# The first batch of a delta-net kernel: rounds of two and four tiles, state per head half, smaller transfers

## The chip, the cores and the metric

The kernel runs on one core of a Trainium2 chip. A core has five engines that run side by side: TensorE (PE, matrix products), VectorE (DVE), ScalarE (ACT), GpSimd (POOL) and SyncE (SP, which here only issues DMAs). TensorE reads from the on-chip memory SBUF and writes into PSUM, which has eight banks; VectorE and ScalarE copy its results back ("evictions"). DMAs bring data from the main memory. The metric is the time of one execution on the device in microseconds (us); less is better.

## The reference

Two blocks follow one another. The first is a delta-rule attention over 4 batches of 8 heads, 768 positions and a head width of 48; the state of a head is 48 x 48:

```python
k_n = k / (np.linalg.norm(k, axis=-1, keepdims=True) + 1e-06)
for t in range(S):
    kt, vt, bt = (k_n[:, :, t], v[:, :, t], beta[:, :, t, None])
    y[:, :, t] = np.einsum('bhd,bhde->bhe', q[:, :, t], state)
    v_old = np.einsum('bhde,bhd->bhe', state, kt)
    state = state + bt[:, :, :, None] * np.einsum('bhd,bhe->bhde', kt, vt - v_old)
```

The second takes the heads side by side as rows of 384, mixes them, and adds an MLP of width 1536:

```python
X = np.fft.fft(x, axis=1)
X = np.fft.fft(X, axis=2)
u = x + np.real(X).astype(np.float32)
un = (u - mu) / np.sqrt(var + 1e-06)        # mean and variance over the 384
ch = np.maximum(un @ w_ch1, 0.0) @ w_ch2
return (u + ch).astype(np.float32)
```

The weights come as 64-bit floats, and the kernel makes 32-bit ones of them on the chip.

## The kernel before

**Tiles.** A batch has 6 tiles of 128 positions, in all 24 *units*. A unit holds two chunks of 64 positions, one in partitions 0 to 63, the other in 64 to 127. For each unit the keys are transposed (`turn`, L571 in the profile), multiplied with themselves (`keys` for the first batch), and a triangular matrix per head is inverted. The inversion runs on VectorE over a whole *round* of units at once: the 32 x 32 matrices of up to four units lie side by side, and its cost is that of four, however many there are. The first batch has two rounds, units 0 to 3 and 4 and 5; all others have three units. For the first batch `begin16` (L876 to L942) transposes a round's blocks (L902), takes norms on ScalarE (L909, L911), scales (L928), masks (L935), and `invert16` makes 14 steps of a product (L962) and a sum (L968), a scaling (L981) and transpositions back (L986, L990). `join` and `blocks` put the inverse together per unit.

**The chain of the first batch.** `chain0` goes through 12 chunks one after the other. A chunk subtracts the state's product from its values (`f1`), copies the values out (`g1`), adds their products with the keys to the state in its own PSUM bank (`f2`, bank `bS`), and copies the state out (`g2`) for the next chunk. `fq` and `outputs0` make the outputs. State and values are *joined* here: the state of two heads is kept as one 128 x 96 block with zeros off its diagonal (`so_`, in the tile R1), the values of both chunks as one block (`ub_`, in the tiles u and st), so a product covers two heads, or two chunks, at once. The zeros are cleared once on POOL.

**Mixing and MLP.** When the last tile of a batch is done, `mixing` folds the rows, multiplies with tables for the Fourier transform (`tab`, `ft`), normalizes, and the MLP follows in 12 groups of 2.6 us on TensorE for two tiles. `weights` loads the 64-bit weights in 18 pieces of 512 columns, through buffers in ws, x and R, and converts each in six operations on ScalarE (L2017, L2023), VectorE (L2020, L2028, L2036) and POOL (L2033).

**The order of the work.** Nothing runs in the order of the program text. Each operation is recorded (`Plan.op`) with its engines, an estimated duration, a due time and what it reads and writes. `Plan.schedule` then plays the kernel through on the host and fixes one order for each engine; the engines run these orders in sequence and wait for one another by semaphores. Constants at the top of the file (`GAP`, `FORCE`, `LIM`, `START`, `LATER` and others) steer its choices, and `KEYS` gives small shifts to the due times, a number for every 64 operations. Where TensorE has no work ready, `schedule` puts in *fillers*, matmuls with unused results: up to `E2` = 5 us groups of six 64-column ones (L2263), later one of 256 columns or two (L2270). They are placed only up to `D1`, and where fewer columns than `TARGET` a microsecond were streamed over the last `SPANW` us, or nothing is ready within `GAP`; after `D1` only if nothing is ready. `fetch` estimates when the next 256 instructions of TensorE are there; `crowd` gives its delay by transfers. `pace` ties DMAs on SP's queue to an instruction before them.

The lines that all operations share: L568 is every matmul, L571 every transposition, L577, L579 and L581 every plain copy by ScalarE and VectorE, and L615 every load.

## Time and profile before

| | |
|---|---|
| median of 3 runs | 649.18 us (648.48 to 651.63) |
| profiled execution | 648.84 us, its span 647.0 us |
| TensorE busy | 632.9 us (98%) |
| VectorE busy | 507.3 us (78%) |
| ScalarE busy | 271.6 us (42%) |
| moved by DMA | 31.98 MB |

The profile's page gives for one execution the busy time of each engine, the span in 40 slices, the DMA queues, the chain of work that ended last, and the costliest groups of instructions. PE is TensorE's multiplying, PEld its loading of the stationary operand; a matmul of 32-bit floats shows as two records of each kind. A busy PE need not do useful work: fillers count as well. "Granted clock" is the share of TensorE's full clock. A group's row gives line, engine, operation, output and inputs with shapes, count, busy time and the mean of one in ns.

### The profile page before, as it was taken

The page shows a single profiled execution, that of the slowest core. Times are in us where ns is not written, and L with a number is a line of the kernel's source. Part 1 is how long each engine was busy: PE and PEld are TensorE (multiplying, and loading weights), DVE is VectorE, ACT ScalarE, POOL GpSimd, SP SyncE. Part 2 cuts the span into 40 slices and gives each one's busy share as a digit, 9 for nine tenths or more (in the row PEclk, how much of TensorE's full clock was granted, in tenths as well). Part 3 has the DMA queues.
Part 4 walks back from the last instruction along what each step waited for, and adds up shares of the span by engine and source line. Part 5 has one row for each costly group of instructions (what it writes and reads, how often), then busy time and mean ns, then how long its engine had stood idle before and what let it go on. Part 6 is the DMA issues. An engine that isn't in the chain of part 4 may idle for free.

```text
span 647.0 us, 22705 instructions
## 1 busy us (share of the span) xinstructions
PE 632.9 (98%) x9748; PEld 516.6 (80%) x9748; DVE 507.3 (78%) x1529; ACT 271.6 (42%) x804; POOL 39.8 (6%) x44
## 2 busy tenths in 40 slices
PE   9998899999999999999999999999999999999998
PEld 8788788777777877877777777877777699899997
DVE  4998779999997379999863899999828633976573
ACT  3769665543154544421655333345442113321120
POOL 4103313230000000000000000000000000000000
PEclk9999889999999999999999999999999999999999
DMA  6654534550013231000323220000000000000000
GB/s 126 142 161 134 123 100 110 135 152 2 25 28 87 54 64 27 25 1 2 71 46 64 52 51 2 23 5 3 3 27 3 2 24 1 26 2 25 2 25 24
DMA packets 82808, 31.98 MB, mean 49 GB/s; under 512 B 75667, under 2 KB 79732, under 8 KB 82580
## 3 DMA queue, kind: packets, MB, share of 16 engines
q1 hardware_dynamic: 82516, 30.31, 19.3%
q8 instruction: 76, 1.25, 0.8%
q10 hardware_dynamic: 192, 0.23, 0.2%
q14 instruction: 24, 0.20, 0.1%
HBM read 25.81 MB, written 4.72 MB: 47 GB/s over the span
## 4 chain that ended last, share of the span: by engine, by line
PE 77%; DVE 15%; ACT 4%; issue 2%; DMA 1%; DVEq 0%; ACTq 0%
PE pp L568 72%; PE pp L571 3%; DVE rr L1056 2%; DVE tmp L1051 2%; PE pp L2270 1%; PE pp L2263 1%; ACT us L577 1%; DMA ws<-in_moe_w_ch_dram 1%; DVE gd L812 1%; DVE w L968 1%; ACT w L2017 1%; DVE tmp L962 1%; DVE R L1453 1%; DVE rr L902 1%; DVE w L2036 1%
## 5 line engine op out<-in xcount | busy, mean ns | idle before, releaser
L568 PE MATMUL pp<-R,w 128*128 128x256 f32 (+1 forms) x832 | 182.2, 367 | 0.7 <-DVE us L789 0.7
L568 PEld LDWEIGHTS pp<-R,w 128*128 128x128 f32 x832 | 145.6, 190 | 20.2 <-DVE us L789 0.9
L568 PE MATMUL pp<-w,R 128*128 128x384 f32 x384 | 134.6, 495 | 0.0
L577 ACT ACTIVATE us<-pp 32x128 f32<-32x128 f32 (+3 forms) x232 | 73.1, 348 | 87.4 <-PE pp L568 65.2
L568 PEld LDWEIGHTS pp<-w,R 128*128 128x128 f32 x384 | 70.2, 190 | 41.3
L1697 ACT ACTIVATE R<-pp 128x512 f32<-128x512 f32 x47 | 28.1, 597 | 102.3 <-PE pp L568 92.8
L568 PE MATMUL pp<-us 64*64 64x64 f32 (+4 forms) x2784 | 67.1, 231 | 0.0
L568 PEld LDWEIGHTS pp<-us 64*64 64x64 f32 (+2 forms) x2784 | 56.9, 132 | 5.8 <-issue 3.2
L1056 DVE TENSOR_TENSOR rr<-rr,tmp 128x84 f32<-128x84 f32 (+13 forms) x180 | 57.7, 335 | 1.5
L1051 DVE TENSOR_TENSOR tmp<-rr 128x84 f32<-128x84 f32 (+14 forms) x180 | 57.2, 332 | 1.4
L577 ACT ACTIVATE R<-pp 128x192 f32<-128x192 f32 (+8 forms) x103 | 29.7, 332 | 29.5 <-PE pp L568 18.4
L568 PEld LDWEIGHTS pp<-u,us 64*64 64x64 f32 (+2 forms) x1248 | 29.0, 129 | 15.6 <-issue 10.2
L577 ACT ACTIVATE x<-pp 64x192 f32<-64x192 f32 x91 | 28.3, 323 | 27.4 <-PE pp L568 24.0
L1362 DVE TENSOR_TENSOR u<-u,pp 64x192 f32<-64x192 f32 x66 | 22.1, 349 | 18.8 <-PE pp L568 14.5
L1391 DVE TENSOR_TENSOR st<-st,pp 128x192 f32<-128x192 f32 x30 | 10.5, 351 | 33.5 <-PE pp L568 30.4
L1872 DVE TENSOR_TENSOR us<-us,pp 128x256 f32<-128x256 f32 x64 | 26.8, 420 | 12.3 <-ACT us L577 10.8
L2270 PE MATMUL pp<-pack 64*64 64x256 f32 (+1 forms) x198 | 35.0, 396 | 0.1
L568 PE MATMUL pp<-u,us 64*64 64x48 f32 (+3 forms) x1248 | 34.5, 217 | 0.0
L568 PE MATMUL pp<-st,us 48*64 48x48 f32 (+2 forms) x1184 | 29.5, 223 | 2.6 <-issue 1.1
L568 PEld LDWEIGHTS pp<-st,us 48*64 48x64 f32 (+2 forms) x1184 | 25.0, 135 | 8.3 <-issue 4.9
L1828 DVE TENSOR_TENSOR gd<-us 128x128 f32<-128x128 f32 x48 | 11.8, 289 | 21.8 <-ACT us L1904 15.4
L568 PE MATMUL pp<-us,gd 128*128 128x192 f32 x144 | 27.8, 327 | 0.0
(176 smaller groups left out, 999.6 us busy)
## 6 DMA issues: line engine op xcount, KB each, us to landing
out_dram<-x SPq DMA_DIRECT2D x11, 384.0 KB
us<-in_k_dram SPq DMA_DIRECT2D x16, 192.0 KB
us<-in_q_dram SPq DMA_DIRECT2D x16, 192.0 KB
us<-in_v_dram SPq DMA_DIRECT2D x16, 192.0 KB
us<-in_k_dram SPq DMA_DIRECT2D x8, 181.5 KB
us<-in_q_dram SPq DMA_DIRECT2D x8, 181.5 KB
us<-in_v_dram SPq DMA_DIRECT2D x8, 181.5 KB
x<-in_moe_w_ch_dram SPq DMA_DIRECT2D x3, 484.0 KB
```

What stands on the lines that cost most here:

```text
L568: I(nc.tensor.matmul(o, lhsT=lhsT, rhs=rhs, start=start, stop=stop, skip_group_check=True))
L571: I(nc.tensor.matmul(o, lhsT=src, rhs=ident[p0:p0 + n, p0:p0 + n], is_transpose=True, start=start, stop=True, skip_group_check=True))
L577: I(nc.scalar.activation(o, i, ACT.Copy, **({} if scale is None else {"scale": scale})))
L812: I(nc.vector.scalar_tensor_tensor(w[0], w[1], (m1, m0)[s], w[2], op0=ALU.mult, op1=ALU.add))
L1051: I(eng(e).tensor_tensor(T_, R[:, :, j + 1:32, j:j + 1].broadcast_to([128, ns, n, j]), R[:, :, j:j + 1, 0:j].broadcast_to([128, ns, n, j]) ...
L1056: I(eng(e).tensor_tensor(R[:, :, j + 1:32, 0:j], R[:, :, j + 1:32, 0:j], T_, op=ALU.add))
L1362: I(nc.vector.tensor_tensor(U[:, s], U[:, s], psum(b1[s])[a, s0:s1].rearrange("p (j d) -> p j d", d=D), op=ALU.subtract))
L1391: I(nc.vector.tensor_tensor(sn[:, s0:s1], so[:, s0:s1], psum(b2)[:, s0:s1], op=ALU.add))
L1697: I(nc.scalar.activation(o, s, ACT.Relu))
L1828: vec(128, lambda e, j=j, i0=i0, i1=i1, op=op: I(nc.vector.tensor_tensor(s(j), i0, i1, op=op)), [aH] + rd, [aS(j)], pr - P.ev)
L1872: vec(256, lambda e: I(nc.vector.tensor_tensor(o, i0(), i1(), op=ALU.add)), [], [aH] + list(wr), pr - P.ev, use=n)
L2270: I(nc.tensor.matmul(pst[two[0]][x, 0:256], lhsT=w[x, 0:n], rhs=w[x, 0:256], start=True, stop=True, skip_group_check=True))
```

## The change

The first batch's rounds become units 0 and 1, and units 2 to 5. The state and the values are no longer joined: each head has its 48 x 48 state, two heads of a pair lie in the two halves of the partitions, and products are taken head by head; a chunk's state is copied out by one copy of 128 partitions instead of two of 64, the outputs of a tile by two copies instead of four. In `begin16` the mask is applied before the scale. The zeros in w1 and w2 are cleared in three pieces, and the blocks `GF` of units 2 to 5 lie in w2, those of units 0 and 1 in w1. The table is loaded in four transfers of 32 partitions, the weights in pieces of at most 256 columns (`CUT`). In the planner an opening filler is estimated longer and denser, transfers to start earlier (`MOVED`, `SOON`), `crowd` has another form, the operations that the splits add do not shift the numbering of `KEYS` (`extra`), and nearly all constants and all `KEYS` have new values. With them the opening has two groups of fillers.

```diff
-KEYS = [200, 0, 229, 328, 801, 352, 821, 0, 842, 785, 803, 67, 960, 0, 214, 0, 515, 0, 672, 136, 248, 318, 992, 108, 919, 0, 112, 914, 121, 808, 205, 0, 783, 131, 491, 744, 856, 533, 168, 25, 743, 718, 0, 282, 642, 114, 361, 40]
+KEYS = [0, 196, 0, 882, 0, 533, 747, 349, 300, 92, 0, 631, 0, 118, 229, 329, 112, 81, 189, 0, 488, 857, 205, 426, 209, 734, 514, 433, 0, 264, 416, 0, 634, 135, 91, 0, 140, 556, 752, 279, 934, 886, 297, 564, 670, 480, 0, 737]
...
-LOOK, EARLY = 1e9, 19.0271
-FOLD, BY, SEQ, HOT, HOTPE, HOTPK, HOTG, NORM = 1, 1, 1, 1.7459, 0, 0, 0, 1
-HOTC, PORT, E2 = 1, 1, 5.0
-GAP, HALF = 0.3228, 84.0008
+LOOK, EARLY = 1e9, 0.6403
+FOLD, BY, SEQ, HOT, HOTPE, HOTPK, HOTG, NORM = 1, 1, 10, 5.6131, 8, 12, 1, 1
+HOTC, PORT, E2 = 2, 1, 5.0
+GAP, HALF = 0.2477, 85.6671
...
-FORCE = 621.6309
-BLOCK, LEAD, SEEK, LAND, LAND2, HOLDUP = 256, 60, 1.0, 2.3968, 1.964, 1.8
-PACE, PGAP, MOVED = 3.8256, -0.0594, 1.6
-PACED, AHEAD = 6.0, 0.4
-CUT, ROW = 512, 121
+FORCE = -320.3215
+BLOCK, LEAD, SEEK, LAND, LAND2, HOLDUP = 256, 60, 1.0, 2.0432, 1.8604, 1.0
+PACE, PGAP, MOVED = 6.0, -0.4268, -0.7
+PACED, AHEAD, SOON = 6.0, 0.4, 0.8
+CUT, ROW = 256, 121
...
-TARGET, SPANW = 745.8691, 1.1196
-E0, E1, D1 = 1.0, 10.0, 105.9979
+TARGET, SPANW = 768.6683, 4.0822
+E0, E1, D1 = 1.0, 10.0, 266.9663
...
-        return min(1.0, sum(max(0.0, min(z, t + 1.5) - max(a, t - 0.5)) for a, z in self.bursts) / 2.0)
+        return min(2.6, 0.55 * max([0.0] + [z - t for a, z in self.bursts]))
...
-                        best.engs, best.new, best.banks, best.succ = {"PE": 0.432}, [], [], []
+                        best.engs, best.new, best.banks, best.succ = {"PE": 0.65 if now < E2 else 0.432}, [], [], []
...
-            g, go = (w2, 2304 + 512 * u) if u < 4 else (w1, 3584 + 512 * (u - 4))
+            g, go = (w1, 3584 + 512 * u) if u < 2 else (w2, 2304 + 512 * (u - 2))
...
+        def mask(e):
+            I(nc.vector.tensor_tensor(DB, RB, tri[:, None].broadcast_to(sh), op=ALU.mult))
+        vec(512, mask, [aTRI, aR], [aD], pr, port=True)
...
-        def mask(e):
-            I(nc.vector.tensor_tensor(DB, DB, tri[:, None].broadcast_to(sh), op=ALU.mult))
-        vec(512, mask, [aTRI], [aD], pr, port=True)
...
         if n and 0 in part:
             def f1(e):
-                for j in order:
-                    y, k = j // 2, 64 * (2 * j % 4)
-                    mm(psum(z.bU[c])[64 * y:64 * y + 64, k:k + 128].rearrange(
-                        "p (s d) -> p s d", s=2)[:, :, 16 * y:16 * y + D], z.TK[:, c, j, :],
-                       so[:, 96 * j:96 * j + 96].rearrange("p (s d) -> p s d", s=2), False)
+                for j, s, r in jj:
+                    y = 64 * (c ^ s)
+                    mm(psum(z.bU[s])[y:y + 64, 64 * j:64 * j + 64], z.TK[r, c, j, :],
+                       so[r, D * j - wide(j):D * j - wide(j) + 64], False)
...
-        for s in range(2):
-            def g2(e, s=s):
-                w = psum(bS)[64 * s:64 * s + 64, 0:256]
-                copy(e, sn[64 * s:64 * s + 64, :].rearrange(
...
+        P.op(narrow(W), lambda e: copy(
+            e, sn.rearrange("p (i j d) -> p i j d", i=2, d=D), own0(bS)), [], [A(sn, 0, W)],
+             pr - P.ev - 5, use=[bS], lat=LA)
...
-    rounds = [units[0:4], units[4:6]] + [units[6 + sum(SIZES[:i]):6 + sum(SIZES[:i + 1])] for i in range(len(SIZES))]
+    rounds = [units[0:2], units[2:6]] + [units[6 + sum(SIZES[:i]):6 + sum(SIZES[:i + 1])] for i in range(len(SIZES))]
...
-    for i, (w, n) in enumerate(((w2, 4352), (w1, 4608))):
-        c0 = 3584 if i == 1 else 0
+    for i, (w, c0, n) in enumerate(((w2, 0, 2048), (w1, 3584, 4608), (w2, 2304, 4352))):
+        if i == 2:
+            P.extra.append(len(P.ops))
...
-    for t in ub_ + tuple(so_):
-        nk = t.shape[1]
-        P.op({"POOL": 0.1 + 1.0e-3 * nk}, lambda e, t=t: I(eng(e).memset(t, 0.0)), [], [A(t, 0, nk)], -20,
-             lat=LP)
...
-    dma(tab, cn["tab"].ap().rearrange("p t c -> p (t c)"), [A(tab, 0, 1)], 0, kb=1180)
+    for x in range(0, 128, 32):
+        if x:
+            P.extra.append(len(P.ops))
+        dma(tab[x:x + 32], cn["tab"].ap().rearrange("p t c -> p (t c)")[x:x + 32], [A(tab, 0, 1, x, x + 32)], 0,
+            kb=295)
```

More of the change, by code (lines that the diff above doesn't have):

```diff
@@ L511 @@
     ws = sb("ws", 1024)
[L512 to L513 removed]
+    us_ = [sb(f"u{i}", DM) for i in range(3)]
     lo_ = [sb(f"lo{i}", 256) for i in range(2)]
@@ L593, in either, with narrow @@
         return {"ACT": t_act(n) + w, "DVE": t_dve(n) + 0.06}
+    def narrow(n):
+        return {"ACT": t_act(n) + 0.10, "DVE": t_dve(n) + 0.09}
     T_IN, T_EIGHT, T_RATE = 2.0, 8, 170.0
@@ L1263, in chain0 @@
-            P.op({"PE": T_FQ}, fq, [z.aQT(), A(so, 0, DM)] + ([A(sn, 0, DM)] if n > 1 else []),
-                 [], pr - 4, "64", new=z.bO, lat=LE, col=1536, ni=32)
-            P.op({"ACT": 0.08, "DVE": 0.1}, lambda e: copy(
-                e, mv_[0][:, 14:15], psum(z.bO)[:, 0:1]), [], [A(mv_[0], 14, 15)], pr - P.ev,
-                 use=[z.bO], lat=LA)
+                for j, s, r in jj:
+                    for y, t in ((1, so), (0, sp)):
+                        if 2 * z.T + y:
+                            mm(psum(z.bO[s])[64 * y:64 * y + 64, 64 * j:64 * j + 64],
+                               z.QK[r, 0, y, j, :], t[r, D * j - wide(j):D * j - wide(j) + 64],
+                               j == 0)
@@ L1268, in chain0 @@
+            P.op({"PE": 0.55}, fq, [z.aQT(), A(so, 0, W)] + ([A(sp, 0, W)] if n > 1 else []),
+                 [], pr - 4, "64", new=z.bO, lat=LE, col=1024, ni=64)
+            for s in range(2):
+                P.op({"ACT": 0.08, "DVE": 0.1}, lambda e, s=s: copy(
+                    e, mv_[s][:, 14:15], psum(z.bO[s])[:, 0:1]), [], [A(mv_[s], 14, 15)], pr - P.ev,
+                     use=[z.bO[s]], lat=LA)
         if n and 0 in part:
             def f1(e):
-                for j in order:
-                    y, k = j // 2, 64 * (2 * j % 4)
-                    mm(psum(z.bU[c])[64 * y:64 * y + 64, k:k + 128].rearrange(
-                        "p (s d) -> p s d", s=2)[:, :, 16 * y:16 * y + D], z.TK[:, c, j, :],
-                       so[:, 96 * j:96 * j + 96].rearrange("p (s d) -> p s d", s=2), False)
```

161 lines of the change are left out of this document (73 added, 88 removed).

## The prediction

> **What bounds the kernel now.** I read the page first, then the busy time by stage, the chain of work that ended last, and single groups.
>
> ```profile
> span 647.0 us, 22705 instructions
> PE 632.9 (98%) x9748; PEld 516.6 (80%) x9748; DVE 507.3 (78%) x1529; ACT 271.6 (42%) x804; POOL 39.8 (6%) x44
> ```
> ```profile
> 24.60:37.00 12.40, 12.20 (x280) 8.60 (x279) 12.40 (x67) 5.75 (x20) 1.87 (x6) 1.00 0.68 154
> ...
> 75.00:90.00 15.00, 13.28 (x276) 11.03 (x273) 8.91 (x22) 10.07 (x27) 5.65 (x3) 0.77 0.43 104
> ...
> 102.00:121.00 19.00, 17.70 (x165) 15.86 (x164) 18.81 (x53) 10.01 (x30) 4.17 (x2) 1.00 0.53 126
> ```
> ```profile
> 121.00:267.00 146.00, 144.49 (x2330) 109.68 (x2323) 125.64 (x354) 62.89 (x186) 9.87 (x8) 1.00 0.25 58
> 121.00:647.00 526.00, 520.04 (x7312) 420.69 (x7304) 406.14 (x1208) 191.31 (x569) 10.49 (x10) 1.00 0.13 31
> ```
>
> Columns of the stages: from and to; then length, and busy time (and instructions) of PE, its weight loads, VectorE, ScalarE and POOL; granted clock, DMA share, GB/s. After 121 us TensorE is busy for 520.0 of 526 us: that stage is its own work and moves only if the orders leave more or fewer holes. Before 121 us PE also reads as busy, but much of it is filler that keeps the clock up (below), while VectorE is full at 24.6 to 37 us and again at 102 to 121 us. So the time is the fixed 526 us plus whenever the front lets the first MLP matmul go. The front is where this change works. Its chain:
>
> ```profile
> 1.18 7.20 PE pp L2263 x84
> 8.38 0.39 PE pp L571 x8
> 8.77 0.49 PE pp L2078 x6
> ...
> 10.32 0.39 PE pp L571 x8
> 10.71 0.62 PE pp L568 x32
> ...
> 14.83 0.45 ACT gd L577
> ...
> 16.11 0.49 DVE gd L748
> 16.62 1.96 DVE rr L902
> ...
> 21.91 0.68 DVE w L928 x2
> ...
> 22.93 0.55 DVE w L935
> ...
> 35.10 0.67 DVE w L981 x2
> 35.90 0.98 DVE gd L986
> ```
>
> Columns: start, duration, what. The chain starts with 84 filler matmuls (line 2263) that last 7.20 us; the first real work, the transposition of tile 0's keys (L571), starts when they are through. Nothing was waited for there but the filler in front of it in TensorE's queue.
>
> **The change, part by part.** *Two opening filler groups.* A group is 6 matmuls, 12 records, so 84 records are 7 groups. Is tile 0's key block there earlier? Bytes by microsecond:
>
> ```profile
> 2.00:3.00 1.00, 1.00 (x12) 1.00 (x12) 0.82 (x6) 0.99 (x2) 1.00 (x3) 1.00 0.87 206
> 3.00:4.00 1.00, 1.00 (x12) 1.00 (x11) 0.00 (x0) 0.17 (x1) 1.00 (x1) 1.00 1.22 296
> ```
> ```profile
> 1.00:6.00 5.00, 4.82 (x47) 4.82 (x47) 1.00 0.91 187
> 6.00:8.00 2.00, 2.00 (x38) 2.00 (x37) 1.00 1.07 214
> ```
> ```profile
> us<-in_k_dram SPq DMA_DIRECT2D x16, 192.0 KB
> pack<-k_pack ACTq DMA_DIRECT2D x1, 130.0 KB
> x<-in_beta_dram ACTq DMA_DIRECT2D x1, 96.0 KB
> ```
>
> Identity table, beta and tile 0's keys are 418 KB; 26 KB (of the microsecond before these rows) plus 206 plus 63% of 296 make that at about 3.6 us. From the last byte to the release I allow 1 us (no row shows it; 0 to 3 are the bounds): 4.6 us. The second fence is the fillers alone (line 2263): 47 in 4.82 us, 103 ns each, until 6 us, then 38 in 2.00, 53 ns. The clock was at half until about 6 us although the granted clock reads 1.00. Two groups, 24 at 103 ns, end at 1.18 + 2.5 = 3.7 us, so the keys now set the start: 4.6 instead of 8.38. But TensorE is then cold, and the real work doubles: two turns 0.78 each, beta 0.98, two key products 1.24 each, 5.0 in all, to 9.6 us. The same products of tiles 0 and 1 end in the chain above at 10.71 + 0.62 + 0.39 + 0.62 = 12.3 (tile 2's turn stands between them). Gain 2.7. The other four tiles at 1.01 each end at 13.6 where they ended at 16.5 (row below, 15.34 + 1.16): 2.9. If the cold state lasted through all six, they would cost 4 us more and this gain would turn into a loss of 1; if it were warm, 5.
>
> ```profile
> 15.34 1.16 PE L568 MATMUL pp<-us 48*64 48x64 f32 x64
> ```
>
> The rule that speaks against fewer fillers is the Trainium skill's, TensorE: Matmul & The Clock Gate, What's actually happening: half rate by default, full rate after a busy window of some 3.4 us, and half rate again after an idle one. The trace agrees in size: a mean clock of 0.77 over 15 us is 6.9 us at half rate, two such windows. By that rule the opening could stay cold for one window more, 3.4 us longer than the 4.6 us start suggests; the estimate by it would be about 1.7 us less gain.
>
> *Rounds of two and four; mask first.* A round's inversion on VectorE costs the same for any number of tiles up to four:
>
> ```profile
> L968 DVE TENSOR_TENSOR w<-w,tmp 128x28 f32<-128x28 f32 (+6 forms) x28 | 5.8, 243 | 0.0
> L962 DVE TENSOR_TENSOR tmp<-w 128x28 f32<-128x28 f32 (+6 forms) x28 | 5.8, 242 | 0.0
> ```
>
> 11.6 us for both rounds, 5.8 for one. Now they run interleaved and the first block to be joined is there at 36.9 us. The first round needs four tiles' keys before its transposition at 16.62; a round of two needs two: 9.6 plus two evictions on ScalarE (L577, 0.45 each) and, beginning behind the first, two on VectorE (L748, 0.49 each), 11.4 if they follow one another with nothing between. From there 1.96 for the transposition; an allowance of 1.2 for the root and reciprocal, whose tiny instructions lie hidden in the chain (from its end at 18.58 to the scale at 21.91 at most, 3.3, most of which VectorE spent on the other round); 0.68 for the scale; the mask, 0.55, has moved ahead of it and now runs during the root; 5.8; 0.67; 0.98: the first joinable block at 22.7 alone, at 29 if the second round's own evictions (4 x 0.49), transposition, scale, mask and a turn's copies or two, about 6, go between, against 36.9. The second round's end depends on VectorE's total, which is the same; it moves by the 2.8 that the opening gives. The path into the MLP lies between 2.8 (VectorE full to the end) and 8 (the chain of tiles alone). I take 4, near the lower bound, since VectorE is full in the row 24.6 to 37.
>
> *Unjoined state.* Per tile, 4 value copies, 4 state copies (two per step), 4 output copies and a probe become 4, 2, 2 and two probes. PE's passes are twice as many and half as wide; I cost them at 0 (bounds -2 and +2): 8 records of 128x96 take 0.55 us, 16 of 64x64 about as long (0.68).
>
> ```profile
> 67.50 0.55 PE L568 MATMUL pp<-R 128*64 128x96 f32 x8
> 68.22 0.68 PE L568 MATMUL pp<-t,us 64*64 64x64 f32 x16 [0.17 <-ACT R L577]
> ```
> ```profile
> L577 ACT ACTIVATE R<-pp 64x192 f32<-64x192 f32 x20 | 6.5, 324 | 2.1 <-PE pp L568 1.7
> ```
> ```profile
> L579 DVE COPY st<-pp 64x192 f32<-64x192 f32 x6 | 2.1, 355 | 2.1 <-PE pp L568 2.0
> ```
>
> A copy costs 0.324 on ScalarE and 0.355 on VectorE, and I take the same for 128 partitions of 192 (bounds one and two of them). Over six tiles 70 copies become 47, and 6 more probes of one column are left out as small: 23 x 0.33 = 7.6 us of both engines. Of the copies in these two rows VectorE has 6 of 26: its share is 1.8. On the chain of steps the state's two copies, mostly on one engine one behind the other, become one: 11 x 0.33 = 3.6. Between 1.8 and 3.6 I take 2.7.
>
> *Smaller transfers.* Weight pieces of 256 columns instead of 512 make 24 more issues on SP's queue, the table in four 3 more. 27 at 0.29 are 7.9 us, spread over 110 us in which the queue mostly waits for its pacing.
>
> ```profile
> L615 SPq DMA_DIRECT2D x<-in_moe_w_ch_dram x24: 268/291/328, 38.5 to 133.7; - x24
> L615 SPq DMA_DIRECT2D tab<-k_tab x2: 421/539/657, 52.2 to 139.8; - x2
> ...
> L568 PEld LDWEIGHTS pp<-tab,R x48: 160/163/164, 94.5 to 109.2; 128*96 128x96 f32 x24, 128*97 128x97 f32 x12, 128*95 128x95 f32 x12
> ```
>
> The table is issued at 52.2 and first read at 94.5: hidden. I cost this part at 0; without its cover, 7.9. One case of a late transfer is in the trace, and shows the price of a stall:
>
> ```profile
> 76.03 0.66 ACT L2017 ACTIVATE w<-ws 128x512 f32<-128x512 f32 x1 [2.45 <-DMA ws<-in_moe_w_ch_dram]
> ```
>
> ScalarE waited 2.45 us for weights with the next state copy queued behind it, TensorE for that copy, and the clock fell: 13.28 us busy at 0.77 is 3.1 lost. Together some 5 us. A new order may miss it or meet another; 0, bounds -5 and +5.
>
> The Trainium skill, DMA: Bandwidth & Descriptors, Bandwidth, asks for transfers of 1 MiB and more and gives each a fixed 2 us; paid one after the other, 27 of them would be an estimated 54 us. The trace does not bear out that they add: the opening's key blocks, 192 KB each, came at 187 GB/s over 1 to 6 us, first latency included, and at 214 over 6 to 8, queued one behind the other.
>
> *The rest.* Four clears on POOL go, the clear of w2 is cut in two, the filler slots move between w1 and w2: POOL is 6% busy, 0. *Orders anew* for the long stage: its holes are 6.0 us of idle and 8.8 us of fillers (line 2270 below), so -7 at best; I take 0.
>
> Sum: 4.0 + 2.7 = 6.7, from the profiled run's 648.84 (span 647.0 and 1.84 around it; 0.34 under the median): 642.1, so 642.
>
> **The rivals.** *The front is given back.* The MLP starts when the last work of a full VectorE and the paced weights are through; both are placed by the order, not by the chain. For it: 18.81 of 19 us at 102 to 121. Against: VectorE is idle for over 6 of the 15 us at 75 to 90. Then only the copies' 1.8 come, and less: 647 to 649.
>
> *Fillers in the long stage (slower).* The filler window now reaches to 267 us instead of 106, and its measure is 4.1 us long. Rows of line 2270:
>
> ```profile
> 110.00:121.00 11.00, 2.65 (x8) 1.20 (x8) 1.00 0.53 136
> 121.00:647.00 526.00, 8.80 (x32) 5.42 (x32) 1.00 0.13 31
> ```
>
> Fillers in front of ready work cost what they last. At the rate of 110 to 121 us, 146 us would hold 35 us of them; against this, PE has only 1.5 us of holes there, so the measure should seldom ask. Half of it, 17.5, gives 660; it decides from a fifth on, 6.7 us, where the gain is used up. With a third, 11.7, the time is 654.
>
> *Weights late (slower).* The 7.9 us of added issues come in front of the last pieces, and the gain is lost with them: 657. Against: the queue's pacing leaves room.
>
> **How the numbers follow.** Forecast 0.58; given back 0.18; fillers or a worse order of the long stage 0.16; weights late 0.08. About 0.5% (3.2 us) is what a measurement can tell from no change: below 645.9 is faster, above 652.4 slower. Some of the forecast's mass lies in that band and a little of the given-back case beyond it: faster 0.58, same 0.2, slower 0.22. The forecast's own range is 634 (chain in full, 8 + 3.6, and no stall) to 646 (opening cold, copies 1.8); with the slower cases up to 655.
>
> **What would show it.** 24 opening fillers; first L571 before 5.5 us; first L902 near 11; the first L986 before 30; copies of 128x192 for the state; first MLP matmul (128x256, of the weights) near 114 instead of 121; the same 526 us behind it. Wrong if the turns start late in spite of fewer fillers (landing, not queue), if the clock stays low past 12 us, or if fillers of line 2270 show behind 121 us.

## The result, and the profile after

The changed kernel took 645.01 us (median of 13 runs, 640.33 to 648.18), the kernel before 648.96 (13 runs, 646.76 to 651.63). The ratio is 0.9933, 95% interval 0.9905 to 0.9961: some 4 us faster, where 6.7 were forecast. The ratios leave out executions more than 1.5% above the fastest of their kernel (three in all, in the experiment with fewer fillers). The profiled execution took 647.48 us with a span of 645.6, so it is one of the slower ones: its span is only 1.4 us shorter than the 647.0 before. On two other chips, in the experiments below, the same kernel had 0.9894 (0.9858 to 0.9929) and 0.9857 (0.9817 to 0.9898). The first and the last of these intervals do not overlap, and single executions lie 10 us apart (637.7 to 648.2): that spread has to be explained along with the gain.

Line numbers have moved a little: L568 is now L561 (matmuls), L571 is L564 (transpositions), L577 and L579 are L570 and L572 (copies), L2263 and L2270 are L2260 and L2267 (fillers), L902 and L986 are L895 and L979, L2017 is L2013 (weights).

The opening on TensorE, from the timeline of the changed kernel (start, duration, engine, line, operation, tiles, shapes, count, and in brackets the wait):

```profile
1.18 2.82 PE L2260 MATMUL pp<-pb 128*64 128x64 f32 x24 [1.18 <-DVE pb L686]
4.51 0.69 PE L564 MATMUL pp<-pack,us 64*128 64x64 f32 x8 [0.50 <-DMA us<-in_k_dram]
...
5.90 1.54 PE L2260 MATMUL pp<-pb 128*64 128x64 f32 x12
...
7.99 1.13 PE L561 MATMUL pp<-us 48*64 48x64 f32 x32
...
16.70 1.13 PE L561 MATMUL pp<-us 48*64 48x64 f32 x32
...
18.46 1.06 PE L561 MATMUL pp<-us 48*64 48x64 f32 x28
```

The 24 fillers are there, and the first turn starts at 4.51 after a wait for the load, as forecast (4.6). A third opening group, of 12 records, stands behind the first turn and beta (the third row), where the text on the change counts two groups in all. But a key product takes 1.13 us all the way to 19.5, against 0.69 in the same view of the kernel before: the clock, which was to be released near 9.6, stays at half. The last pair's products end at 19.5 instead of 16.5.

To account for the rest I use two marks: the first copy of a chunk's values (u from pp, the entry into the chain of states) and the first MLP matmul. Both, before and then after:

```profile
49.52 0.72 DVE L579 COPY u<-pp 64x192 f32<-64x192 f32 x2
```
```profile
121.22 5.45 PE L568 MATMUL pp<-R,w 128*128 128x256 f32 x24
```
```profile
46.29 0.37 DVE L572 COPY u<-pp 64x192 f32<-64x192 f32 x1
```
```profile
116.53 5.34 PE L561 MATMUL pp<-R,w 128*128 128x256 f32 x24
```

The entry is 3.23 earlier. From there to the MLP it is 70.24 instead of 71.70, 1.46 less. From the MLP's start to the end of the span it is 529.1 instead of 525.8, 3.3 more. Together 1.4, the difference of the spans.

Two places inside show where it went. ScalarE waits for weights with a state copy queued behind it, and TensorE for that copy (first fence: timeline of ScalarE; second: TensorE's waits from 40 to 121 us, as total, times, longest):

```profile
73.31 0.67 ACT L2013 ACTIVATE w<-ws 128x512 f32<-128x512 f32 x1 [3.45 <-DMA ws<-in_moe_w_ch_dram]
```
```profile
PE pp L561 <- ACT st L570: 3.3, 1, 3.3
PE pp L561 <- issue: 3.0, 5, 0.8
```

And in the long stage TensorE stops in the middle of a gram product, with nothing to wait for that the profile shows, and the clock falls behind it (stages: length, busy times, then granted clock, DMA share, GB/s):

```profile
204.07 1.40 PE L561 MATMUL pp<-us 48*64 48x128 f32 x48 [1.65 <-issue]
```
```profile
200.00:205.00 5.00, 3.35 (x194) 3.01 (x191) 3.31 (x10) 2.92 (x10) 0.00 (x0) 0.97 0.67 161
205.00:215.00 10.00, 10.00 (x280) 8.41 (x276) 2.68 (x8) 5.20 (x18) 0.00 (x0) 0.67 0.13 26
```

Ten microseconds at 0.67 are 3.3 lost, and the wait adds 1.65. The whole stage is only 3.3 longer, so a part of it is made good elsewhere. In the same stretch the kernel before had a clock of 1.00 and no hole.

### The profile page after: what moved, and what is told of

Same layout as the page of the kernel before. It is cut to its first block, busy times and chain, and to the rows that moved or that the text cites. A ratio compares the mean times of both kernels' runs of the same rounds, so it can differ in the third digit from the quotient of the medians.

```text
span 645.6 us, 23067 instructions
## 1 busy us (share of the span) xinstructions
PE 625.0 (97%) x9900; PEld 511.9 (79%) x9900; DVE 512.1 (79%) x1524; ACT 269.0 (42%) x791; POOL 35.9 (6%) x42
## 3 DMA queue, kind: packets, MB, share of 16 engines
q1 hardware_dynamic: 84742, 30.31, 19.3%
## 4 chain that ended last, share of the span: by engine, by line
PE 77%; DVE 15%; DMA 3%; ACT 2%; issue 2%; SPq 0%; DVEq 0%; ACTq 0%
PE pp L561 71%; PE pp L564 3%; PE pp L2267 3%; DVE tmp L1044 3%; DVE rr L1049 3%; ACT us L570 1%; DMA us<-in_k_dram 1%; DVE w L2032 1%; DVE us L782 1%; DVE gd L805 1%; DVE rr L851 1%; DVE R L1449 1%; DMA ws<-in_moe_w_ch_dram 1%; DMA x<-in_moe_w_ch_dram 1%; DMA tab<-k_tab 1%
## 5 line engine op out<-in xcount | busy, mean ns | idle before, releaser
L561 PE MATMUL pp<-R,w 128*128 128x256 f32 (+1 forms) x832 | 184.7, 370 | 0.2 <-DVE us L782 0.2
L561 PEld LDWEIGHTS pp<-R,w 128*128 128x128 f32 x832 | 146.9, 192 | 19.6 <-DVE us L782 0.3
L561 PE MATMUL pp<-w,R 128*128 128x384 f32 x384 | 134.8, 494 | 0.0
L570 ACT ACTIVATE us<-pp 32x128 f32<-32x128 f32 (+3 forms) x240 | 75.9, 349 | 81.0 <-PE pp L561 58.0
L561 PEld LDWEIGHTS pp<-w,R 128*128 128x128 f32 x384 | 69.9, 190 | 40.7 <-issue 0.2
L561 PE MATMUL pp<-us 64*64 64x64 f32 (+4 forms) x2784 | 70.4, 236 | 2.2 <-issue 1.6
L561 PEld LDWEIGHTS pp<-us 64*64 64x64 f32 (+2 forms) x2784 | 59.9, 138 | 8.2 <-issue 3.3
L1044 DVE TENSOR_TENSOR tmp<-rr 128x30 f32<-128x30 f32 (+9 forms) x180 | 58.0, 331 | 2.0
L1049 DVE TENSOR_TENSOR rr<-rr,tmp 128x108 f32<-128x108 f32 (+9 forms) x180 | 57.0, 325 | 2.0
L561 PEld LDWEIGHTS pp<-u,us 64*64 64x64 f32 (+1 forms) x1472 | 37.5, 132 | 17.5 <-issue 10.3
L561 PE MATMUL pp<-u,us 64*64 64x48 f32 (+2 forms) x1472 | 43.9, 219 | 2.2 <-issue 1.6
L570 ACT ACTIVATE R<-pp 128x192 f32<-128x192 f32 (+6 forms) x82 | 22.8, 336 | 31.0 <-PE pp L564 19.6
L561 PE MATMUL pp<-st,us 48*64 48x48 f32 (+1 forms) x1232 | 28.7, 224 | 2.3 <-issue 0.8
L561 PEld LDWEIGHTS pp<-st,us 48*64 48x64 f32 x1232 | 24.3, 136 | 8.0 <-issue 4.3
L570 ACT ACTIVATE x<-pp 64x192 f32<-64x192 f32 (+1 forms) x78 | 24.0, 323 | 15.4 <-PE pp L561 13.0
L570 ACT ACTIVATE u<-pp 64x192 f32<-64x192 f32 (+1 forms) x71 | 23.2, 326 | 15.6 <-PE pp L561 11.3
L561 PE MATMUL pp<-us,gd 128*128 128x192 f32 x144 | 27.8, 327 | 0.0
L1424 DVE TENSOR_TENSOR x<-x,pp 64x192 f32<-64x192 f32 x66 | 23.2, 352 | 4.6 <-PE pp L561 2.8
```

The source lines that it names most:

```text
L561: I(nc.tensor.matmul(o, lhsT=lhsT, rhs=rhs, start=start, stop=stop, skip_group_check=True))
L570: I(nc.scalar.activation(o, i, ACT.Copy, **({} if scale is None else {"scale": scale})))
L1044: I(eng(e).tensor_tensor(T_, R[:, :, j + 1:32, j:j + 1].broadcast_to([128, ns, n, j]), R[:, :, j:j + 1, 0:j].broadcast_to([128, ns, n, j]) ...
L1049: I(eng(e).tensor_tensor(R[:, :, j + 1:32, 0:j], R[:, :, j + 1:32, 0:j], T_, op=ALU.add))
L1424: I(nc.vector.tensor_tensor(w, w, v, op=ALU.add))
```

## The experiments

All compare with the kernel before on their own chip. The kernels below that move operations do it in the finished order, so that nothing else is planned anew.

**The changed kernel again, twice.** No edit.

> The changed kernel once more, for a second profile. If the 1.65 us of issue wait in the gram products near 202 and the clock of 0.50 to 0.84 behind it belong to this order of work (three loads of 384, 192 and 192 KB issued within 3.4 us, with the fetch of instructions behind them), a wait of 1 us or more stands again within 201 to 205 and the stretch 205 to 215 has a clock under 0.9. If they are chance of the one execution, they are gone, and the span is some 3 to 5 us shorter with the first MLP matmul unchanged near 116.5. The wait of ScalarE for the weights at 70 (3.45 us) is expected again within 1 us in either case.

> The changed kernel a third time, beside the two kernels below on the same chip. One of two openings is expected: clock released near 4.6, key products of the last pair ended at 13.7, first state copy at 43.7; or not released before 17, 19.3 and 49.1. The times of its executions spread over 5 us or more, between 638 and 648.

Measured: 641.16 us (637.86 to 644.69), and 639.94 (637.73 to 641.94); the spread of the latter is 4.2 us, not 5 or more. The opening of the first repetition:

```profile
4.26 0.53 PE L564 MATMUL pp<-pack,us 64*128 64x64 f32 x8 [0.25 <-DMA us<-in_k_dram]
...
6.44 0.69 PE L561 MATMUL pp<-us 48*64 48x64 f32 x32
...
13.22 0.69 PE L561 MATMUL pp<-us 48*64 48x64 f32 x32 [0.55 <-DVE us L572]
```
```profile
40.89 0.34 DVE L572 COPY u<-pp 64x192 f32<-64x192 f32 x1
```
```profile
110.06 5.34 PE L561 MATMUL pp<-R,w 128*128 128x256 f32 x24
```

The same program, but here the clock was released within the first turn, and key products take 0.69 instead of 1.13 from 6.4 on. The chain is entered at 40.89, 5.4 earlier than in the first profile and 8.6 earlier than before, and the MLP starts at 110.06. The third profile had the slow opening again (last key product ended at 19.3) and entered the chain at 45.24. The hole in the gram products stood in both, with 1.38 and 1.37 us, so it belongs to the order; but it stood there without the drop of the clock behind it, which the first expectation had with it: from the MLP to the end 526.4 and 526.6 us.

**Fewer fillers in the kernel before.** Five of its seven opening groups are taken out of the order:

```diff
     P.pace()
+    first = [o for o in P.order if o.i == -1 and o.start < E2]
+    for o in first[2:]:
+        P.order.remove(o)
```

> The kernel before with two of its seven opening filler groups; everything else in its place: the opening part of the change alone. Theory A: first turn near 4.6 instead of 8.31, at the low clock, and the key products of the last pair end near 19 instead of 16.5; first transposition 2 to 4 us earlier than 16.6, second round 2 to 3 us later than 19.4; time within 1 us of the kernel before, or up to 3 us slower. Rival C (the prediction's: the clock is released near 9.6 whatever fills the time): key products end near 13.6, and the time is some 3 us under the kernel before.

Measured: 653.01 us against 648.26 (ratio 1.0059, 1.0032 to 1.0085): slower. Its profiled execution (657.58 us) is among its slowest, so only the opening is read from it:

```profile
4.13 0.69 PE L571 MATMUL pp<-pack,us 64*128 64x64 f32 x8
...
13.20 1.13 PE L568 MATMUL pp<-us 48*64 48x64 f32 x32
...
16.02 1.99 PE L568 MATMUL pp<-us 48*64 48x64 f32 x64
```

The clock stayed at half, and the last key products end at 18.0 instead of 16.5. Rival C, the prediction's release near 9.6, is refuted here. Theory A was wrong about VectorE's transpositions. The first did not come earlier, but at 16.6 as before: a round of four waits for four tiles, whose key products start earlier, are slower, and end at 14.3, where they ended before; and the second, at 19.5 for 19.4, did not come later. The loss is 3.8 us by the ratio (2.1 to 5.5), where it allowed 3; where it arises was not followed. So the opening part of the change alone gains nothing. The round of two with key products as late as before follows below.

**Longer fillers in the changed kernel.** The second group is made 192 or 256 columns wide, with the same number of instructions:

```diff
             if now < E2:
+                n = 192 if 2.0 < now < 3.0 else 64        # or 256
                 for i in range(6):
-                    I(nc.tensor.matmul(pst[two[0]][0:64, 64 * i:64 * i + 64], lhsT=w[:, 0:64],
-                                       rhs=w[:, 64:128], start=True, stop=True,
+                    I(nc.tensor.matmul(pst[two[0]][0:64, 0:n], lhsT=w[:, 0:64],
+                                       rhs=w[:, 0:n], start=True, stop=True,
```

> The second opening filler group with 192 columns instead of 64, nothing else. Theory A (the opening of the changed kernel is slow because 2.8 us of fillers end before the clock is released, and the narrow turns and key products do not release it): fillers last to about 6.2, the first turn comes near 6.3 instead of 4.51 but takes 0.40 instead of 0.62, the key products 0.62 instead of 1.06, those of the last pair end near 15 to 16 instead of 19.5, the second round's first transposition comes near 18.5 instead of 21.8, and the time is 1 to 3 us under that of the changed kernel. Rival B (the start of the MLP hangs on VectorE and the paced loads, whatever the opening does): the key products end earlier as in A, the first MLP matmul stays within 1 us of 116.5 and the time within 1 us of the changed kernel's.

> The second opening filler group with 256 columns instead of 64, nothing else: at the low clock the fillers then last from 1.2 to some 8.2 us, and end earlier if the clock is released before. Theory A2 (whether the clock is released in the opening depends on where the fillers fall in time, which differs between executions of the same kernel: released at 4.6 in the second profile of the changed kernel, not before 19 in the first; 7 us of fillers always do): first turn at 6 to 8, 0.39 us pitch, key products of the last pair end at 15 to 17, first state copy near 46 (43.7 with the clock released, 49.1 without, in the two profiles), and the times of the executions lie within 4 us of one another (the changed kernel's 7 us), with a median between 638 and 642. Rival (chance elsewhere makes the spread): the spread stays at 6 us or more.

Measured: 641.21 us (636.0 to 644.17; ratio 0.9881, 0.9847 to 0.9915) with 192 and 642.46 (641.43 to 644.11; 0.9912, 0.9886 to 0.9939) with 256. From the timeline with 256:

```profile
1.18 5.82 PE L2261 MATMUL pp<-pb 128*64 128x64 f32 x24 [1.18 <-DVE pb L686]
6.93 0.46 PE L564 MATMUL pp<-pack,us 64*128 64x64 f32 x8
...
15.83 0.70 PE L561 MATMUL pp<-us 48*64 48x64 f32 x32 [0.54 <-DVE us L572]
```
```profile
43.44 0.36 DVE L572 COPY u<-pp 64x192 f32<-64x192 f32 x1
```

The fillers themselves tell when the clock was released, by the starts of the single records in the traces. At half clock a record of 64 columns starts 0.107 us after the one before it, one of 192 columns 0.320 and one of 256 columns 0.427; at the full clock the wide ones follow at 0.163 and 0.216. The step changes at 6.0 us with 256 columns and at 4.6 with 192; in the five kernels below that have a wide group it changes at 4.3, 4.4, 4.5, 6.0 and 6.8. So in every profile with a wide second group, seven in all, the clock was released while the fillers ran. With 2.82 us of fillers (and in the kernel above) it was released early once in five profiles; in the other four the step of the wide fillers behind the key products changes only at 19.3 to 20.9. The early releases come 3.1 to 5.6 us after the first filler, and not at a fixed place. The Trainium skill, TensorE: Matmul & The Clock Gate, What's actually happening, says that a window of 3.4 us runs freely and does not start with the kernel; the 2.5 us between the earliest and the latest of these releases agree. It also says that the release therefore varies by half a microsecond either way. Here the measurement differs: what misses it in the opening gets it some 15 us later. In those four profiles the turns, the key products and the short fillers between them did not release the clock, however closely they stand; whether their kind or their place in time is the reason was not tried.

Three things follow. With 256 columns the last key products end at 16.53, the same place as before (16.50), and yet the chain is entered at 43.44 instead of 49.52. So 6.1 us of the front's gain come from what stands behind the key products (the rounds, the mask, the new order, not tried apart), and the short fillers add 2.6 (40.89) or take 2.9 (46.29) by chance.

The time does not follow the entry. With 192 columns it is 641.21, beside the changed kernel's 641.16 on the same chip: the key products end earlier, as theory A has it, but the 1 to 3 us are not there. In the time rival B is right, though the MLP starts at 114.0 and not within 1 us of 116.5. One reason is in the profile. The piece of weights does not come earlier by as much as the chain does, and TensorE's wait for the state copy behind it grows, here with 192 columns:

```profile
PE pp L561 <- ACT st L570: 4.4, 1, 4.4
```

In the four kernels with a wide group, one state copy and this wait left in, the wait is 3.2 to 4.5 us and 69.9 to 72.5 pass from entry to MLP; in the three profiles of the changed kernel it is 2.3 to 3.3 and 68.4 to 70.2.

The spread hangs on the opening in part: with 256 columns the six executions lie within 2.7 us, though their median lies a little above the 642 expected. With 192 they lie 8 us apart in spite of the early release in the one that was profiled; the two fastest (636.0, 638.0) have a mean granted clock of 1.000 and 0.999, the other four 0.989 to 0.997. What goes with such drops is seen below.

**Weights later on ScalarE.** ScalarE's passes over the piece it waits for, and the next, are put 4 to 6 us later in the order, VectorE's behind them (the numbers are operations; each is put behind the second one):

```diff
     P.pace()
+    behind(537, 340)    # |hi|, ScalarE
+    behind(538, 498)
+    behind(539, 417)    # low word, ScalarE
+    behind(540, 532)
+    behind(547, 408)    # the same two passes of the next piece
+    behind(549, 379)
```

> The changed kernel with the two ScalarE passes over the weight piece that it waited 3.45 us for, and those over the next piece, put 4 to 6 us later in the program order, with the four VectorE passes behind them. Theory D (the wait holds up the state and value copies queued behind it, and the clock drops with it): the wait at 70 to 73 goes or falls under 0.5 us, the clock stays 1.00 from 70 to 80, the last state product comes 3 to 4 us earlier than 93.8, the first MLP matmul near 113 instead of 116.5, and the time is 2 to 4 us under the changed kernel's. Rival E (the weights themselves set the first MLP matmul): the wait goes, the state chain ends earlier, the first MLP matmul stays near 116.5 and the time within 1 us.

Measured: 639.07 us (635.64 to 644.95; ratio 0.9869, 0.9833 to 0.9905), against 641.16 for the changed kernel on the same chip. TensorE's waits from 40 to 121 us:

```profile
PE pp L561 <- issue: 2.5, 3, 1.1
PE pp L561 <- DVE R L1449: 0.5, 1, 0.5
```

The wait for the state copy is gone, the clock is 1.00 from 60 to 121 us, and from the entry to the MLP it is 66.29 us (46.73 to 113.02) where the three profiles of the changed kernel have 70.24, 69.17 and 68.38. The opening was the slow one and the MLP started at 113.02, as theory D had it. That the weights set the MLP's start (rival E) does not fit: they were converted later, and the MLP came 2.1 to 4.0 us sooner after the entry. The times show 2 us with intervals that overlap, and this is one profile; the two kernels at the end bear on it again.

**The state copied in two halves.** The two-copy form of the kernel before, on top of the 256-column fillers:

```diff
-        P.op(narrow(W), lambda e: copy(
-            e, sn.rearrange("p (i j d) -> p i j d", i=2, d=D), own0(bS)), [], [A(sn, 0, W)],
+        def g2(e):
+            for p in (0, 64):
+                copy(e, sn.rearrange("p (i j d) -> p i j d", i=2, d=D)[p:p + 64],
+                     own0(bS, p, p + 64))
+        P.op(narrow(W), g2, [], [A(sn, 0, W)],
              pr - P.ev - 5, use=[bS], lat=LA)
```

> As fill_long, and the copy of the state out of its bank done as two copies of 64 partitions, one behind the other on the engine that had it. Theory A (each of the eleven copies stands on the chain of state products): one copy of 64x192 takes some 0.32 us, so the chain from the first state copy to the last product gets 11 x 0.33 = 3.6 us longer and the time 2.5 to 4 us. Rival F (ScalarE and VectorE hide it, since other work stands between the products): chain and time within 1 us of fill_long.

Measured: 645.37 us (642.12 to 646.94; ratio 0.9940, 0.9918 to 0.9963) against 642.46 (0.9912, 0.9886 to 0.9939), 2.9 more; the intervals overlap. The copies, first in the changed kernel and then here (count, then the shortest, the median and the longest in ns, the first and the last start):

```profile
L570 ACT ACTIVATE st<-pp x10: 323/331/338, 49.1 to 92.1; 128x192 f32<-128x192 f32 x10
L572 DVE COPY st<-pp x1: 358/358/358, 61.7 to 61.7; 128x192 f32<-128x192 f32 x1
```
```profile
L570 ACT ACTIVATE st<-pp x20: 308/324/326, 45.3 to 92.9; 64x192 f32<-64x192 f32 x20
L572 DVE COPY st<-pp x2: 341/350/360, 58.6 to 59.0; 64x192 f32<-64x192 f32 x2
```

A copy of 128 partitions costs what one of 64 does. From entry to MLP it is 74.48 us instead of 69.93; 1.2 of the 4.55 are the wait for weights, 4.4 here and 3.2 there. The 3.35 left are close to 11 x 0.33 = 3.6, but that is one pair of profiles. From the start of one state copy to the next, ten profiles with one copy have 2.91 to 2.95 us in the first of the ten steps, 2.53 to 2.54 in the fourth and 3.79 to 3.86 in the fifth; here they are 3.53, 2.81 and 4.14. In the third (6.24), the ninth (3.81) and the tenth (4.32) it lies within the others. So the state copy stands on the chain with its full length in some steps for certain, and rival F falls; that it does so in all is not shown.

**Larger transfers.** Also on top of the 256-column fillers: the table goes in one transfer, pieces of the first weight in 512 columns; each sits where the first of its parts was, and the other parts are dropped.

```diff
         def fn(e):
+            if whole is not None:              # one dict for all the parts of a piece
+                if "all" not in whole:
+                    whole["all"] = 1
+                    I(nc.sync.dma_start(out=whole["o"], in_=whole["i"]))
+                return
```

> As fill_long, with the table loaded in one transfer at the place of the first of its four, and the pieces of the first MLP weight in transfers of 512 columns at the place of the first of their two; the second MLP weight's pieces are left in parts. The prediction's step (smaller transfers: 0): time within 1 us of fill_long. Rival G (smaller transfers let loads of q, k and v pass between them): waits of PE for us loads of 0.5 us and more come back in 20 to 60, and the time is 1 to 3 us longer. Rival H (the many issues on SP hold up the weights): the waits of ScalarE for weights get shorter and the time 1 to 2 us shorter.

Measured: 644.65 us (640.18 to 646.14), ratio 0.9932 (0.9907 to 0.9958), against 0.9912 with small ones. The intervals overlap. The median is 2.2 us above the kernel with small ones, where the prediction's step allowed 1 and rival G 1 to 3. In the profile no wait for q, k or v comes back and the wait for weights does not get shorter (3.7), so neither rival's mechanism is seen. This profile also has a hole of 1.92 us near 200 with the clock behind it. Smaller transfers cost nothing that can be seen; whether they gain 1 or 2 us stays open. The fixed 2 us that the prediction sets against them stand in the Trainium skill, DMA: Bandwidth & Descriptors, under Anatomy of one DMA — SWDGE (gpsimd) path, for transfers that GpSimd issues; here SP issues them.

**The first result sent later.** On top of the 256-column fillers, the 384 KB that go out before 200 us are put behind four loads on SP's queue, and a load of q and one of v are put later:

```diff
     P.pace()
+    behind(1522, 1058, True)    # load of q
+    behind(1523, 1522)
+    behind(814, 1063)           # the result, 384 KB
+    behind(1729, 1073, True)    # load of v
```

> As fill_long, with the transfer of the first result (384 KB) moved behind four loads in SP's queue, the load of q some 2 us and that of one v 9 us later. Theory I (the wait of 0.8 to 1.65 us within the gram products near 200 is the fetch of instructions behind that transfer): the wait falls under 0.3 us, the clock from 198 to 215 is 1.00, and the time is 1 to 3 us under fill_long's. Rival J (the wait belongs to the amount of code there, whatever moves on the queues): the wait stays at 0.8 or more and the time within 1 us.

Measured: 643.09 us (639.98 to 644.22; ratio 0.9906, 0.9877 to 0.9935). The transfer now starts behind the hole, and the hole is still there:

```profile
203.53 0.41 SPq L1661 DMA_DIRECT2D out_dram<-x  x1
```
```profile
203.13 1.12 PE L561 MATMUL pp<-us 48*64 48x128 f32 x48 [0.83 <-issue]
```

So theory I falls: without the transfer in front of it the wait is still there. The hole has the same place in the program in all eleven profiles that have this order (behind the first 15 or 16 of the 64 records of one gram product, 0.82 to 1.92 us long), while the order before has none there.

What it is can be read from the traces. Count every record of TensorE, matmuls, weight loads and those of its sequencer, from the first one on. In the thirteen profiles of this document 53 waits of 0.5 us or more are put down to "issue", and in front of every one of them stand 193 or 194 records, or that many and a multiple of 256: they recur by blocks of 256, and nowhere else. Instructions come over a queue of their own; the page of the changed kernel, busy row and queue row:

```profile
PE 625.0 (97%) x9900; PEld 511.9 (79%) x9900; DVE 512.1 (79%) x1524; ACT 269.0 (42%) x791; POOL 35.9 (6%) x42
q8 instruction: 78, 1.28, 0.8%
```

That is 78 packets of 16 KB for some 19,900 records, one for each 256, and each of the 53 waits ends 1.1 to 1.6 us after the end of one of these packets. So TensorE stood there for its next block of instructions. The kernel before with 120 records taken out bears it out: its waits, at 218.5 and 475.1 us, again stand at block borders, while the full order has its only one at 317.2. Near 200 the two blocks in front of the hole are used up in 4.5 us, the fastest pair in any of the profiles (others take some 6 or more): the amount of code, as rival J has it, and the time stays within 1 us of 642.46. The length of the hole goes with the packet: where it took 0.93 to 1.30 us the hole has 0.82 to 1.08, where it took 1.41 to 1.81 the hole has 1.10 to 1.92, and in one (256 columns, weights later) a short packet started late. So transfers beside it may lengthen the hole, but no run set that. What the hole goes with is seen across the profiles:

| profile | entry of the chain | first MLP matmul | from there to the end | hole near 200 |
|---|---|---|---|---|
| before | 49.52 | 121.22 | 525.8 | none |
| after | 46.29 | 116.53 | 529.1 | 1.65 |
| after, again | 40.89 | 110.06 | 526.4 | 1.38 |
| after, third | 45.24 | 113.62 | 526.6 | 1.37 |
| 192 columns | 42.16 | 114.01 | 528.3 | 1.60 |
| 256 columns | 43.44 | 113.37 | 526.2 | 1.08 |
| two copies | 42.50 | 116.98 | 526.4 | 0.84 |
| larger transfers | 41.62 | 114.11 | 528.6 | 1.92 |
| result later | 43.84 | 115.89 | 526.5 | 0.83 |
| weights later | 46.73 | 113.02 | 526.6 | 0.82 |
| 256, weights later | 42.43 | 111.91 | 529.8 | 1.65 |
| 192, weights later | 41.51 | 109.82 | 525.8 | 1.10 |

Where the hole is 1.38 or less the rest takes 525.8 to 526.6, as before; where it is 1.60 or more, 528.3 to 529.8, and only in those four does the clock fall below 0.9 somewhere between 200 and 215. Two of them:

```profile
200.00:215.00 15.00, 14.64 (x472) 12.69 (x475) 6.97 (x18) 11.06 (x35) 0.00 (x0) 1.00 0.35 70
```
```profile
200.00:215.00 15.00, 15.00 (x398) 12.75 (x401) 4.95 (x15) 8.08 (x26) 0.00 (x0) 0.77 0.31 62
```

The first is the first repetition of the changed kernel, the second the kernel with 256 columns and later weights. This goes together in eleven profiles, and no experiment set the length of the hole.

**Both mends together.** Long fillers and the later weight passes.

> The long second filler group of fill_long and the later weight passes of no_stall together. If the two gains stand one behind the other (the opening sets the first state copy, the wait for the weights lies inside the chain of states): first state copy near 46, chain from it to its last product near 42.6 as in no_stall instead of 46.2, first MLP matmul near 110 instead of 113.4, time 638 to 640 and 2.5 to 4 us under fill_long, with executions within 4 us of one another. If the weights set the end of the chain once it starts earlier: a wait of 2 us or more for the weights stands again between 60 and 85, and the time is within 1.5 us of fill_long's 642.5.

> As combo_long with 192 columns in the second filler group, so fillers of 4.5 us if the clock is released early and 6.8 if not. Expected: first state copy near 45 where the clock is released, MLP start near 109, median within 1.5 us of combo_long, either way; single executions without a release would stand out some 5 us above the others.

Measured beside the changed kernel's 639.94: with 256 columns 639.99 us (637.87 to 643.54; ratio 0.9864, 0.9824 to 0.9903), with 192 columns 637.70 (636.86 to 638.98; 0.9828, 0.9792 to 0.9864). The last is the fastest kernel here, 11.7 us under the kernel before on its chip. Five of the six executions of the changed kernel there lie above its slowest; their intervals overlap. Of the expectations, 638 to 640 for 256 columns held, but not executions within 4 us (5.7) nor the MLP near 110 (111.9); 192 columns came 2.3 us below it, not within 1.5. Entry and MLP with 192:

```profile
41.51 0.34 DVE L572 COPY u<-pp 64x192 f32<-64x192 f32 x1
```
```profile
109.82 5.34 PE L561 MATMUL pp<-R,w 128*128 128x256 f32 x24
```

The wait for the state copy is gone in both, but only part of it is gained: with 256 columns 69.48 us pass from entry to MLP, with 192 columns 68.31, not 66.29. What stands there instead, with 256 columns and with 192:

```profile
PE pp L561 <- issue: 5.1, 5, 2.0
```
```profile
PE pp L561 <- issue: 2.3, 1, 2.3
```

These waits, 5.1 and 2.3 us where the changed kernel had 3.0 and the kernel with later weights alone 2.5, stand at block borders too, as far as they last 0.5 us or more. So where the weights no longer hold up the chain, its code does in part; how much of the gain that takes was not tried.

## Why the prediction was right or wrong

The forecast, 642 against 645.0, was right in sign and near in size, and the measured time lies in the range, near its upper end of 646. One of the prediction's own signs of being wrong came true, the low clock past 12 us, and part of the hit is luck. The ends of the range do not come out of the terms beside them either: 8 + 3.6 and a stall of 5 give 632, an opening at a loss of 1 and copies at 1.8 give 648.

- **Opening, a part of the −4.0.** Start of the first turn (4.51 for 4.6) and number of fillers in front of it: right. The step that failed is "to 9.6 us" for the cold clock: in three of four profiles of this opening it lasted to 19 us or more, in the fourth it ended near 4.6. The prediction named both cases, with a loss of 1 and a gain of 5, and put the middle between them, which no profile shows. Both sizes were off as well: the last key products end 3.0 us later than before (19.5) or 2.6 earlier (13.9). The sum had no fillers between the turns, and in front of the fourth key product alone stand rows of 1.54, 1.06 and 1.22 us at half clock (0.91, 0.60 and 0.70 at the full one). By its marks, the first round's transposition came at 12.8 (10.1 with the clock released) for 11.4, and the first block to be joined at 34.2 (28.9) for "before 30".
- **Rounds of two and four, the rest of the −4.0.** The gain was put down to earlier keys, through a path bounded by 2.8 and 8. With key products ended at the same 16.5 as before, the longer fillers still show 6.1 us at the entry of the chain. So what stands behind the keys carries it; the fillers decide by chance about 2.6 more or 2.9 less. The entry is 3.2 and 4.3 us earlier with the slow opening and 8.6 with the fast one. That the first two fit the 4.0 is luck: a gain at the keys that was a loss, and more than forecast behind them. Rounds, mask and order were not tried apart.
- **Unjoined state, −2.7.** From entry to MLP 1.5, 2.5 and 3.3 us less in the three profiles, with a wait of ScalarE for weights inside that is longer than before (2.7 to 3.45 for 2.45). The experiment puts the copies alone at 3.35 in one pair of profiles, near the upper bound of 3.6: the chain, not VectorE's share, was the right view, though only some steps show it for certain.
- **Stall by weights, 0 between −5 and +5, price some 5.** It stayed, 3.45 us on ScalarE and 3.3 on TensorE. Taken away, it gave 2 to 4 us up to the MLP in one profile and about 2 in the time; together with the long fillers, less.
- **Smaller transfers, 0.** Not refuted; 1 or 2 us either way can't be told.
- **Long stage, 0 and "the same 526 us".** Right in seven of the eleven profiles, and off by 2 to 4 us in the others, the first one among them. The prediction had no term for a place in the new order where TensorE uses up its code faster than it comes, and the clock behind it.
- **Rivals.** "The front is given back" fell as a whole: the MLP starts 4.7 to 11.2 us earlier. But a part was given back: with wide fillers an earlier entry met a longer wait behind the weights, and the time stayed. "Weights late", with its 657, fell too. "Fillers in the long stage" fell: the later form of filler, behind 121 us, is 1.73 us instead of 8.80.

```profile
121.00:646.00 525.00, 1.73 (x6) 1.03 (x6) 0.99 0.11 28
```

## What to carry to other kernels

Before an opening is shortened, ask what its fillers buy: here they buy the clock of the next 15 us, and in four of five profiles the work behind them could not buy it. A group that lasts long enough at half clock got the release in all seven profiles (wide matmuls shorten themselves, being half as long once it has come); judge by a number of executions, since one profile shows one of two openings. An earlier start is worth little where the chain then waits longer for something else, as for the weights here. A copy that stands on a chain of dependent steps is worth its full length in each step in which nothing else ends later. And where an engine stops at the same place of its program in every execution, with nothing to wait for, count its instructions: here each such stop fell on a border of 256.

## What the runs showed of the hardware

- In the opening matmuls ran at half rate until past 19 us while the granted clock read 1.00; only the durations show it (1.13 and 0.69 us for one key product).
- Small work in close order did not release the clock: transpositions, 48-row products and short fillers followed one another from 4.5 to 19 us without it, in four profiles of five. When the first of them starts does not decide it: at 4.26 us the clock was released in one profile and not in another.
- A copy out of PSUM by ScalarE took 331 ns for 128 partitions of 192 and 324 ns for 64 (medians).
- TensorE's code came in blocks of 256 instructions (16 KB, 0.9 to 1.8 us each for those near 200 us). All 53 waits of 0.5 us or more with nothing else to wait for fell on a block's border, and ended 1.1 to 1.6 us after a block's packet.
- A hole of 1.6 us or more near 200 us went with a drop of the clock and 2 to 4 us in all; one of 1.4 or less with no drop and no loss that can be seen.
